# A new written order for a single-core kernel: DMA queue, PSUM banks and copy engines of a gated recurrence and its gated convolution layer

## The chip, the cores and the metric

One core of one Trainium2 chip runs the kernel. The time is device microseconds of that core, here as the median of several executions. Beside it stands the span: from the first to the last instruction of one execution that the hardware profiler recorded.

The engines are named as in the profile: PE (TensorE, matrix multiplications; PEld its weight loads), DVE (VectorE), ACT (ScalarE), POOL (GpSimd) and SP (SyncE, which here only issues DMAs). Each engine runs its own instructions in the order in which they were written and waits at semaphores for the others. DMAs are issued by SP in one queue and are carried out by 16 DMA engines.

## The reference

Two stages over x of shape (4, 6336, 256), 25,344 rows of 256 values. The first is a gated linear recurrence over the sequence, the second a layer that gates a projection by a causal convolution of width 5:

```python
sig_r = 1.0 / (1.0 + np.exp(-r_gate)); sig_i = 1.0 / (1.0 + np.exp(-i_gate))
a_t = np.exp(c * sig_r * np.log(a_base))
x_gated = np.sqrt(np.maximum(1.0 - a_t * a_t, 1e-06)) * sig_i * x
for t in range(S):
    h = a_t[:, t] * h + x_gated[:, t]
    y[:, t] = h
...
for k in range(K):
    gate_pre += conv_w[k][None, None, :] * yp[:, k:k + S, :]
out = (1.0 / (1.0 + np.exp(-gate_pre)) * (y @ w_val)) @ w_out
```

## The kernel before

The rows are cut into 51 windows (0 and 1 and 50 of 256 rows, the others of 512) and these into 28 chunks (CHUNKS: chunks 0 to 2, 26 and 27 hold one window, the others two). BATCHES joins chunks for the square root, GROUPS joins them for the transposes of the recurrence gate. All of this is the same before and after.

The schedule is a table of words, ORDER. A word such as `cv.12@6,7` calls the function `op_cv` for window 12 with the PSUM banks 6 and 7 (there are eight banks). The functions are called in the order of the table, so the table sets the order of each engine's instructions, of SP's queue, and which bank each product goes to; nothing else decides it. In the words, the first number is a window for lr, li, lx, pp, up, uv, xp, cv, tg, vl, gv, ou, cd, ca, st; a chunk for ta, tb, tr, ex, sq, sa, nt, xg, xt, sc; a batch for rt. They are:

- SP: `lr`, `li`, `lx` load 512 KB (256 KB for a small window) of r_gate, i_gate and x (L289); `st` stores a window of the output (L513); `s_wl` loads weights. The loads go into rings of four windows each (`place`, and `w % NX` for x), so a load of window w waits until window w-4 has been used: `lr` for `ta`, `li` for `tb`, `lx` for `up`. The output ring has four windows too.
- ACT: `ta` and `tb` the hyperbolic tangents of r and i (L307, L310), `ex` the exponential that gives a (L370), `rt` the square root of one batch (L397), `tg` the tangent of the convolution (L469), `ca` a copy of a finished window out of PSUM (L502), `sa` a square. `rt` needs another function table than the rest; the loop over ORDER puts a table load (L529) at each change.
- POOL: `pp` adds one to tb (L317), `up` multiplies by x (L329), `sq` squares a (L378).
- DVE: `xg` multiplies by the square root (L419), `sc` the scan (L450), `gv` gate times value (L482), `cd` the same copy as `ca` (L500), `uv` for a few windows the work of `up`.
- PE: `tr`, `nt`, `xt`, `xp` transposes (L354, L412, L428, L334), `cv` convolution (L462), `vl` value projection (L477), `ou` output projection (L492).

For one chunk the chain is lr, ta, tr, ex, sq, rt, nt, xg, xt, sc, then for each window cv, tg, gv, ou, a copy, st; and beside it li, tb, pp, up (with lx) into xg, and sc into vl and gv.

Which engine copies a finished window is a word of the table as well: `cd` or `ca`.

```python
            if eng == "D":
                nc.vector.tensor_copy(out=dst, in_=src)
            else:
                nc.scalar.copy(out=dst, in_=src)
...
        for word in ORDER.split():
            word, _, at = word.partition("@")
            name, *idx = word.split(".")
            if table.get(name, have) != have:
                have = table[name]
                nc.scalar.preload_act_table_set(have)
            emit[name](*[int(k) for k in idx], *[int(k) for k in at.split(",") if k])
```

Of the kernel before, what the change touches and what calls it, by code (L numbers as in the profile page):

```python
# [33 lines left out]
GROUPS = [[0], [1], [2], [3, 4], [5, 6], [7, 8], [9, 10], [11], [12], [13, 14], [15, 16], [17, 18], [19, 20], [21], [22],  # L34
    [23, 24], [25], [26], [27]]

ORDER = """
s_ident s_small s_kt s_diag lr.0 ta.0 lr.1 ta.1 li.0 tr.0.1@0 tb.0 pp.0 tr.0.0@1 ex.0.1 tr.1.0@2 tr.1.1@3 lr.2 ta.2
ex.1.0 tr.2.1@0 ex.1.1 ex.2.1 tr.2.0@2 lr.3 lr.4 lr.5 ex.0.0 ta.3 lr.6 ta.4 li.1 tr.3.1@0,1 lx.1 tb.1 sq.2.1 sq.1.1
sq.0.1 ex.2.0 li.2 tr.3.0@2,3 li.4 lx.0 li.3 tb.2 xp.1@4 sq.0.0 sq.1.0 sq.2.0 up.0 uv.1 lr.7 lr.8 ex.3.1 sq.4.1 ex.3.0  # L40
sq.3.0 lr.9 lr.10 lx.2 lx.4 s_wl.2 lx.3 li.5 li.6 s_wl.1 tb.3 s_wl.3 s_wl.0 ta.5 lx.5 ta.6 lr.14 rt.0 xp.2@2,3 nt.0@4
xg.0 xt.0@0,1 li.8 li.7 uv.2 rt.1 rt.2 nt.1@4 nt.2@5 xg.2 xg.1 pp.4 sq.3.1 sq.4.0 lx.6 rt.3 lr.11 tb.4 lr.12
tr.5.0@6,7 ex.5.0 xt.1@5,4 li.9 lr.13 sc.0.0 sc.0.1 pp.3 up.4 lx.8 nt.3@2,3 xt.2@0,1 sc.1.0 li.10 up.3 sc.1.1 xg.3
xt.3@2,3 tb.5 cv.1@4,5 sc.2.1 lx.7 sc.2.0 tg.1 cv.0@6,7 tg.0 tr.5.1@0,1 ex.5.1 s_wcast vl.1@4,5 sc.3.1 sc.3.0 xp.6@6,7
vl.0@0,1 nt.4@2,3 li.12 pp.5 ta.7 lr.16 sq.5.0 sq.6.0 up.5 li.11 ta.8 pp.8 uv.6 tb.6 gv.0 ou.0.0@0 lr.15 cv.2@6,7 tg.2
xg.4 tr.7.1@2,3 ex.7.1 cd.0.0 xt.4@1,0 st.0 gv.1 ou.1.0@4 cd.1.0 pp.7 tr.7.0@6,7 vl.2@4,5 ex.7.0 lx.10 sc.4.1 gv.2
cv.3@2,3 ou.2.0@4,5 vl.4@6,7 st.1 up.8 li.14 lr.18 up.7 sq.6.1 tb.7 lx.9 cd.2.0 tg.3 cv.4@2,3 ta.9 vl.3@4,5 lr.17
sc.4.0 cv.6@0,1 tg.4 gv.4 gv.3 ou.3.0@4,5 sq.7.1 st.2 sq.7.0 lr.20 sq.5.1 pp.12 ou.4.0@6,7 cd.4.0 rt.4 lx.11 li.13
lx.12 lr.19 pp.10 cd.3.0 up.10 st.3 st.4 cv.5@2,3 nt.5@4,5 tg.5 tg.6 xg.5 nt.6@6,7 pp.9 up.9 xg.6 lx.14 li.16 li.15
ta.10 lr.21 lr.22 xt.5@4,5 tb.8 lx.13 sq.8.1 pp.11 ta.11 lr.24 lr.23 vl.5@0,1 tr.9.1@6,7 sc.5.1 ex.9.1 sc.5.0 gv.5  # L50
xt.6@2,3 sc.6.0 tr.9.0@4,5 ex.9.0 vl.6@0,1 li.18 cv.7@6,7 li.17 gv.6 nt.7@4,5 up.11 up.12 tb.9 cv.8@0,1 tg.7 sc.6.1
ta.12 xg.7 ou.5.0@6,7 cd.5.0 tg.8 ou.6.0@2,3 li.20 lx.16 cv.9@4,5 cd.6.0 xt.7@0,1 pp.14 up.14 sq.9.1 pp.13 st.5
vl.7@2,3 sq.9.0 up.13 sc.7.0 ta.13 lx.15 tg.9 tb.10 st.6 li.19 lx.17 tr.12.1@6 vl.9@4,5 gv.7 gv.9 ou.7.0@2,3 cd.7.0
sq.10.1 ou.9.0@4,5 sc.7.1 cd.9.0 cv.10@2,3 lr.25 sq.10.0 sq.8.0 rt.5 pp.17 lr.26 st.7 vl.8@0,1 tr.12.0@7 gv.8 pp.16
nt.8@4,5 xg.8 pp.15 ex.12.1 nt.9@0,1 xt.8@4,5 up.15 up.16 tb.11 xg.9 tg.10 ou.8.0@0,1 ca.8.0 ex.12.0 st.9 lr.27 lx.18
sc.8.1 sc.8.0 tr.11.0@6 ex.11.0 cv.11@2,3 vl.11@0,1 tr.11.1@5 tg.11 gv.11 lx.20 lr.28 st.8 ex.11.1 lx.19 vl.10@6,7
li.21 li.22 xt.9@2,3 up.17 pp.18 pp.20 ta.14 li.24 li.23 cv.12@4,5 tg.12 sq.12.0 pp.19 lx.21 gv.10 sc.9.0 ou.11.0@0,1
# [12 lines left out]
ou.23.0@2,3 ca.23.0 cv.22@0,1 tg.22 pp.27 pp.28 up.27 up.28 st.23 li.33 lx.32 xg.15 sc.14.1 sc.14.0 sq.17.0  # L70
ou.21.0@6,7 ca.21.0 vl.22@2,3 lx.31 xt.15@0,1 gv.22 st.20 tb.17 li.36 li.35 cv.24@6,7 st.21 pp.30 sq.18.0 ta.20
sc.15.0 sc.15.1 sq.18.1 pp.29 cv.26@4,5 tg.24 tg.26 up.30 lr.44 up.29 lx.33 pp.31 sq.17.1 tr.19.0@2,3 ex.19.0
nt.16@6,7 vl.24@4,5 tb.18 xg.16 pp.32 up.32 lx.36 lx.34 tr.19.1@0,1 ou.22.0@2,3 ex.19.1 up.31 xt.16@6,7 gv.24 cd.22.0
cv.25@4,5 tg.25 st.22 sc.16.1 sc.16.0 ou.24.0@2,3 cd.24.0 tb.19 cv.27@0,1 lr.41 vl.26@4,5 gv.26 lr.43 vl.25@6,7
vl.27@2,3 gv.25 sq.19.1 sq.19.0 tg.27 gv.27 st.24 cv.28@0,1 ou.25.0@6,7 cd.25.0 lr.42 ou.26.0@4,5 pp.34 st.25 cd.26.0
ou.27.0@2,3 cd.27.0 rt.8 nt.17@6,7 xg.17 tr.21.1@4 vl.28@2,3 pp.36 tg.28 gv.28 ta.23 ex.21.1 ta.22 xt.17@6,7 sc.17.0
cv.30@0,1 tg.30 pp.33 up.34 sq.20.0 li.37 up.36 pp.35 up.33 lx.35 li.38 nt.18@2,3 sc.17.1 sq.21.1 sq.20.1 vl.30@4,5
tr.21.0@6 ex.21.0 tr.22.0@0 ex.22.0 xg.18 up.35 st.26 li.40 li.39 gv.30 tr.22.1@1 ex.22.1 tb.20 ou.28.0@6,7 xt.18@2,3
sq.22.1 sq.21.0 sq.22.0 cv.29@4,5 tg.29 cv.31@0,1 vl.29@4,5 tg.31 cd.28.0 vl.31@6,7 sc.18.1 sc.18.0 st.27 lx.37 st.28
lr.45 tb.21 lx.38 li.41 pp.40 pp.38 gv.29 lx.39 gv.31 nt.19@0,1 xg.19 lx.40 lr.46 pp.37 pp.39 up.37 up.38 up.39  # L80
ou.29.0@4,5 ou.30.0@2,3 rt.9 cd.30.0 ou.31.0@6,7 cd.31.0 st.30 li.42 cd.29.0 st.29 cv.33@0,1 xt.19@2,3 sc.19.0 sc.19.1
# [22 lines left out]
def kernel(  # L104
# [456 lines left out]
```

## Time and profile before

| | |
|---|---|
| median of 3 runs | 296.16 us (295.24 to 296.34) |
| the profiled execution: its own time | 295.84 us |
| its span | 293.7 us |
| mean granted TensorE clock | 0.988 |
| copies of a window from PSUM, 128x1024 | DVE x31, 1212 ns each; ACT x17, 1021 ns each |
| copies in all (with the small windows) | DVE 33, ACT 18 |
| HBM read, written | 78.39 MB, 25.95 MB |
| a 512 KB load, issue to landing, median | r 7.8, i 7.2, x 7.7 us |

The profile page gives, for the span, how long each engine was busy, then the same in 40 equal slices, the DMA queues, the chain of waits that ended last, and groups of instructions by source line with the idle time before them. A window view gives the same busy times for a stretch that one chooses; a timeline lists instructions with start and length. An engine that is busy for nearly all of a stretch bounds that stretch; where it is idle, what ended its wait is written behind it.

### The profile page before, as it was taken

The page shows a single profiled execution, that of the slowest core. Times are in us where ns is not written, and L with a number is a line of the kernel's source. Part 1 is how long each engine was busy: PE and PEld are TensorE (multiplying, and loading weights), DVE is VectorE, ACT ScalarE, POOL GpSimd, SP SyncE. Part 2 cuts the span into 40 slices and gives each one's busy share as a digit, 9 for nine tenths or more (in the row PEclk, how much of TensorE's full clock was granted, in tenths as well). Part 3 has the DMA queues.
Part 4 walks back from the last instruction along what each step waited for, and adds up shares of the span by engine and source line. Part 5 has one row for each costly group of instructions (what it writes and reads, how often), then busy time and mean ns, then how long its engine had stood idle before and what let it go on. Part 6 is the DMA issues. An engine that isn't in the chain of part 4 may idle for free.

```text
span 293.7 us, 6223 instructions
## 1 busy us (share of the span) xinstructions
PE 237.7 (81%) x2470; PEld 163.7 (56%) x2497; DVE 243.4 (83%) x211; ACT 276.1 (94%) x200; POOL 241.8 (82%) x161
## 2 busy tenths in 40 slices
PE   2263778777697899997969889888889998999993
PEld 1241555445364758566636657556648664767652
DVE  5000797857999899998999998999999999999981
ACT  4899999999999999999999999999999999999754
POOL 1559979999899979999998899999998999565300
PEclk9996899999999999999999999999999999999999
DMA  7899999999999999999998999999999999965336
GB/s 240 310 405 389 382 407 408 413 407 383 402 405 389 394 367 407 394 379 396 413 330 286 370 415 413 421 363 408 378 374 387 381 345 374 352 224 214 148 144 250
DMA packets 29995, 104.75 MB, mean 357 GB/s; under 512 B 3335, under 2 KB 3854, under 8 KB 29966
## 3 DMA queue, kind: packets, MB, share of 16 engines
q1 hardware_dynamic: 29952, 104.35, 92.6%
q8 instruction: 19, 0.31, 0.4%
q14 instruction: 10, 0.08, 0.1%
q10 hardware_dynamic: 14, 0.01, 0.0%
HBM read 78.39 MB, written 25.95 MB: 355 GB/s over the span
## 4 chain that ended last, share of the span: by engine, by line
ACT 33%; PE 20%; DMA 19%; issue 11%; DVE 9%; POOL 3%; SPq 2%; ACTq 0%; DVEq 0%; POOLq 0%
DMA xring<-in_x_dram 10%; ACT ering L397 7%; ACT aring L370 6%; ACT tgring L469 6%; ACT tbring L310 6%; PE banks L477 5%; DMA rring<-in_r_gate_dram 5%; PE banks L492 5%; PE banks L462 4%; ACT taring L307 3%; ACT L529 3%; DVE tgring L482 3%; PE banks L412 3%; DMA out_dram<-oring 3%; DVE oring L500 2%
## 5 line engine op out<-in xcount | busy, mean ns | idle before, releaser
L329 POOL TENSOR_TENSOR uring<-tbring,xring 128x1024 bf16<-128x1024 bf16 (+1 forms) x48 | 100.8, 2114 | 9.2 <-DMA xring<-in_x_dram 8.3
L450 DVE TENSOR_TENSOR_SCAN yring<-aring,yring,banks 128x1024 bf16<-128x1024 f32 (+5 forms) x54 | 106.1, 1988 | 2.1 <-PE banks L428 1.9
L378 POOL TENSOR_TENSOR ering<-aring 128x1024 f32<-128x1024 f32 (+2 forms) x54 | 91.4, 1712 | 10.5 <-ACT aring L370 10.5
L462 PE MATMUL banks<-yring,diag 64*64 64x512 bf16 (+7 forms) x1080 | 62.0, 361 | 4.0 <-ACT tgring L469 1.4
L482 DVE SCALAR_TENSOR_TENSOR tgring<-tgring,banks 128x1024 bf16<-128x1024 bf16 (+1 forms) x51 | 58.9, 1177 | 6.1 <-ACT tgring L469 4.5
L317 POOL TENSOR_SCALAR tbring<-tbring 128x1024 bf16<-128x1024 bf16 (+1 forms) x48 | 48.8, 1028 | 12.2 <-ACT tbring L310 11.9
L492 PE MATMUL banks<-wo,tgring 128*128 128x256 bf16 x396 | 51.1, 274 | 7.3 <-DVE tgring L482 6.3
L370 ACT ACTIVATE aring<-banks,khf 128x2048 f32<-128x2048 bf16 (+3 forms) x38 | 54.4, 1469 | 0.6 <-PE banks L354 0.6
L477 PE MATMUL banks<-yring,wv 128*128 128x512 bf16 (+7 forms) x189 | 47.9, 358 | 6.2 <-ACT tgring L469 2.2
L469 ACT ACTIVATE tgring<-banks 128x1024 bf16<-128x1024 f32 (+1 forms) x51 | 49.6, 1004 | 3.2 <-PE banks L462 3.0
L492 PEld LDWEIGHTS <-tgring 128*128 128x128 bf16 x396 | 41.5, 114 | 17.7 <-DVE tgring L482 12.5
L310 ACT ACTIVATE tbring<-iring 128x2048 bf16<-128x2048 f32 (+2 forms) x28 | 48.1, 1718 | 3.2 <-DMA iring<-in_i_gate_dram 3.2
L307 ACT ACTIVATE taring<-rring 128x2048 bf16<-128x2048 f32 (+2 forms) x28 | 48.0, 1721 | 1.8 <-DMA rring<-in_r_gate_dram 1.7
L397 ACT ACTIVATE ering<-ering 128x4096 bf16<-128x4096 f32 (+5 forms) x15 | 44.7, 3017 | 0.1
L462 PEld LDWEIGHTS <-diag 64*64 64x64 bf16 x1080 | 28.8, 106 | 27.8 <-issue 11.6
L354 PE MATMUL banks<-ident_b,taring 128*128 128x128 bf16 x396 | 30.1, 230 | 16.4 <-ACT taring L307 8.7
L419 DVE TENSOR_TENSOR uring<-banks,uring 128x2048 bf16<-128x2048 bf16 (+2 forms) x28 | 30.3, 1093 | 15.3 <-PE banks L412 14.0
L500 DVE COPY oring<-banks 128x1024 f32<-128x1024 f32 (+1 forms) x33 | 38.2, 1180 | 5.2 <-PE banks L492 5.1
L354 PEld LDWEIGHTS <-taring 128*128 128x128 bf16 x396 | 26.1, 103 | 22.1 <-issue 10.2
L477 PEld LDWEIGHTS <-wv 128*128 128x128 bf16 x216 | 19.5, 97 | 25.9 <-issue 12.6
L412 PE MATMUL banks<-ident,ering 128*128 128x128 f32 x198 | 29.1, 290 | 5.7 <-ACT ering L397 3.2
L412 PEld LDWEIGHTS banks<-ident,ering 128*128 128x128 f32 x198 | 26.0, 207 | 11.2 <-ACT ering L397 6.0
(43 smaller groups left out, 126.3 us busy)
## 6 DMA issues: line engine op xcount, KB each, us to landing
rring<-in_r_gate_dram SPq DMA_DIRECT2D x48, 512.0 KB, 7.8
iring<-in_i_gate_dram SPq DMA_DIRECT2D x48, 512.0 KB, 7.2
xring<-in_x_dram SPq DMA_DIRECT2D x48, 512.0 KB, 7.7
out_dram<-oring SPq DMA_DIRECT2D x48, 512.0 KB, 5.1
rring<-in_r_gate_dram SPq DMA_DIRECT2D x3, 256.0 KB, 3.0
iring<-in_i_gate_dram SPq DMA_DIRECT2D x3, 256.0 KB, 5.4
xring<-in_x_dram SPq DMA_DIRECT2D x3, 256.0 KB, 5.1
out_dram<-oring SPq DMA_DIRECT2D x3, 256.0 KB, 6.4
```

The costliest lines, as they stand in the source:

```text
L310: nc.scalar.activation(**tangent(c, tbring, NTI, iring, NII))
L329: nc.gpsimd.tensor_tensor(out=u, in0=t1, in1=xt, op=ALU.mult)
L370: nc.scalar.activation(out=dst, in_=src, func=ACT.Exp, scale=khf[:, h:h + 1], bias=khf[:, h:h + 1])
L378: nc.gpsimd.tensor_tensor(out=e, in0=a, in1=a, op=ALU.mult)
L397: nc.scalar.activation(out=ering[:].bitcast(BF16)[:, 4 * o:4 * o + 2 * n], in_=ering[:, 2 * o:2 * o + 2 * n], func=ACT.Sqrt, scale=-0.25, ...
L412: nc.tensor.transpose(out=bank[:, k:k + P], in_=ering[:, e + q:e + wins[w] // 2:nq], identity=ident[:])
L450: nc.vector.tensor_tensor_scan(out=yring[:, h, col:col + o1 - o0], data0=aring[:, h, a_at[c] + o0:a_at[c] + o1], data1=xT[:, o0:o1], initi ...
L462: nc.tensor.matmul(out=gp[oh * 64:oh * 64 + 64, h, a:b], lhsT=diag[half * 64:half * 64 + 64, h, k, :], rhs=yring[half * 64:half * 64 + 64, ...
L469: nc.scalar.activation(out=tgring[:, w % NTG, :, 0:wins[w]], in_=live.pop(("gp", w))[:, :, 0:wins[w]], func=ACT.Tanh, scale=0.5)
L477: nc.tensor.matmul(out=val[:, m, a:b], lhsT=wv[:, hk, m * P:(m + 1) * P], rhs=yring[:, hk, col:col + b - a], start=(hk == 0), stop=(hk == ...
L482: nc.vector.scalar_tensor_tensor(out=tgring[:, w % NTG, :, 0:wins[w]], in0=tgring[:, w % NTG, :, 0:wins[w]], scalar=1.0, in1=live.pop(("va ...
L492: nc.tensor.matmul(out=ops[:, j * D:(j + 1) * D], lhsT=gv[:, hk, j:wins[w]:J], rhs=wo[:, hk, :], start=(hk == 0), stop=(hk == H - 1))
```

## The change

ORDER is replaced. It has 961 words before and after, and the same operations on the same windows, with two kinds of difference: the order of the words and the bank numbers behind the @, and the copying engine of five windows. Windows 8, 21, 33 and 35 were copied by ACT (`ca`) and are now copied by DVE (`cd`); window 5 was copied by DVE and is now copied by ACT. So DVE has 36 copies for 33, and ACT 15 for 18. The number of table loads stays 18. CHUNKS, BATCHES and GROUPS are only wrapped differently, so line numbers after them are higher by one. The table, cut to its beginning, its end and the words that the prediction names:

```diff
@@ -31,72 +31,73 @@
 ORDER = """
-s_ident s_small s_kt s_diag lr.0 ta.0 lr.1 ta.1 li.0 tr.0.1@0 tb.0 pp.0 tr.0.0@1 ex.0.1 tr.1.0@2 tr.1.1@3 lr.2 ta.2
-ex.1.0 tr.2.1@0 ex.1.1 ex.2.1 tr.2.0@2 lr.3 lr.4 lr.5 ex.0.0 ta.3 lr.6 ta.4 li.1 tr.3.1@0,1 lx.1 tb.1 sq.2.1 sq.1.1
-sq.0.1 ex.2.0 li.2 tr.3.0@2,3 li.4 lx.0 li.3 tb.2 xp.1@4 sq.0.0 sq.1.0 sq.2.0 up.0 uv.1 lr.7 lr.8 ex.3.1 sq.4.1 ex.3.0
-sq.3.0 lr.9 lr.10 lx.2 lx.4 s_wl.2 lx.3 li.5 li.6 s_wl.1 tb.3 s_wl.3 s_wl.0 ta.5 lx.5 ta.6 lr.14 rt.0 xp.2@2,3 nt.0@4
-xg.0 xt.0@0,1 li.8 li.7 uv.2 rt.1 rt.2 nt.1@4 nt.2@5 xg.2 xg.1 pp.4 sq.3.1 sq.4.0 lx.6 rt.3 lr.11 tb.4 lr.12
...
-cv.3@2,3 ou.2.0@4,5 vl.4@6,7 st.1 up.8 li.14 lr.18 up.7 sq.6.1 tb.7 lx.9 cd.2.0 tg.3 cv.4@2,3 ta.9 vl.3@4,5 lr.17
-sc.4.0 cv.6@0,1 tg.4 gv.4 gv.3 ou.3.0@4,5 sq.7.1 st.2 sq.7.0 lr.20 sq.5.1 pp.12 ou.4.0@6,7 cd.4.0 rt.4 lx.11 li.13
...
-ta.12 xg.7 ou.5.0@6,7 cd.5.0 tg.8 ou.6.0@2,3 li.20 lx.16 cv.9@4,5 cd.6.0 xt.7@0,1 pp.14 up.14 sq.9.1 pp.13 st.5
...
-nt.8@4,5 xg.8 pp.15 ex.12.1 nt.9@0,1 xt.8@4,5 up.15 up.16 tb.11 xg.9 tg.10 ou.8.0@0,1 ca.8.0 ex.12.0 st.9 lr.27 lx.18
...
-ou.21.0@6,7 ca.21.0 vl.22@2,3 lx.31 xt.15@0,1 gv.22 st.20 tb.17 li.36 li.35 cv.24@6,7 st.21 pp.30 sq.18.0 ta.20
...
-tr.23.0@0,1 gv.34 xt.20@4,5 lx.42 tb.23 pp.43 up.41 ex.23.0 ou.33.0@6,7 ca.33.0 sc.20.1 sc.20.0 cv.35@2,3 tg.35
...
-li.45 ta.27 sq.23.0 tr.25.1@0 tr.25.0@1 nt.22@2,3 ca.35.0 up.42 ex.25.0 sq.23.1 lx.44 pp.44 up.44 sq.25.0 sq.24.0
...
-sc.21.0 cv.39@4,5 lx.43 tg.39 up.43 cd.36.0 vl.37@0,1 lx.46 sc.22.0 lx.45 gv.37 rt.10 vl.38@6,7 gv.38 ou.37.0@0,1
-ou.38.0@6,7 sc.22.1 cd.38.0 cv.40@4,5 cd.37.0 tg.40 li.48 vl.39@2,3 gv.39 st.36 nt.23@6,7 pp.46 up.45 up.46 li.47
-tb.25 pp.48 pp.47 lr.49 ta.26 lx.47 st.37 st.38 li.49 li.50 xg.23 vl.40@0,1 gv.40 nt.24@2,3 xg.24 xt.23@6,7 sc.23.1
-ou.39.0@4,5 ca.39.0 tr.27.0@0 tr.27.1@1 ex.27.1 ex.27.0 lx.50 lx.48 cv.42@2,3 up.47 tg.42 st.39 cv.41@4,5 tg.41
-sc.23.0 up.48 ou.40.0@0,1 ca.40.0 st.40 sa.27.1 vl.41@2,3 gv.41 vl.42@4,5 gv.42 tr.26.1@6 sq.27.0 tr.26.0@7 ex.26.0
-xt.24@0,1 sc.24.0 ex.26.1 sq.26.1 sc.24.1 tb.26 pp.49 sq.26.0 ou.41.0@2,3 ca.41.0 cv.43@4,5 cv.44@6,7 vl.43@2,3 tg.43
-ou.42.0@4,5 tg.44 rt.11 st.41 lx.49 nt.25@6,7 ca.42.0 gv.43 vl.44@0,1 xg.25 ou.43.0@2,3 xt.25@6,7 ca.43.0 gv.44
-cv.46@4,5 tb.27 tg.46 cv.45@2,3 tg.45 sc.25.1 sc.25.0 st.42 ou.44.0@0,1 ca.44.0 nt.26@7 st.43 st.44 up.49 xg.26
-vl.46@4,5 gv.46 vl.45@2,3 gv.45 cv.47@0,1 tg.47 ou.46.0@4,5 ca.46.0 xt.26@6,7 sc.26.0 ou.45.0@0,1 vl.47@2,3 ca.45.0
-st.45 nt.27@4 cv.48@5,6 tg.48 sc.26.1 cv.49@0,1 tg.49 gv.47 pp.50 up.50 xg.27 xt.27@5,4 sc.27.1 vl.49@2,3 ou.47.0@6,7
-ca.47.0 st.46 vl.48@0,1 gv.49 ou.49.0@2,3 ca.49.0 sc.27.0 st.47 cv.50@6,7 tg.50 gv.48 st.49 ou.48.0@0,1 ca.48.0 st.48
-vl.50@2,3 gv.50 ou.50.0@2 ca.50.0 st.50
+s_ident s_small s_kt s_diag lr.2 lr.0 s_wl.3 lr.1 li.0 lr.3 s_wl.2 ta.2 ta.0 lr.4 tr.0.1@0 ta.1 lr.6 tr.2.0@1 tb.0
+lr.5 tr.1.0@2 tr.0.0@3 tr.2.1@4 ex.2.0 li.1 tr.1.1@5 li.2 ex.1.1 li.3 ex.0.1 sq.1.1 lx.0 ex.1.0 li.4 sq.2.0 ex.0.0
+ex.2.1 sq.1.0 ta.3 sq.2.1 pp.0 sq.0.0 ta.4 sq.0.1 tb.1 lr.10 tr.3.0@4,5 tb.2 lr.9 lr.8 tr.3.1@2,3 lr.7 ex.3.0 lx.2
+s_wl.1 up.0 lx.1 ex.3.1 sq.3.0 lx.4 lx.3 tb.3 sq.3.1 ta.6 pp.4 sq.4.1 lr.13 ta.5 li.5 li.6 sq.4.0 li.7 xp.2@2,3
+lr.14 pp.3 rt.0 tr.5.0@4,5 lx.6 uv.2 rt.2 up.4 nt.0@0 rt.1 xg.0 rt.3 xt.0@0,1 xp.1@2 sc.0.0 up.3 nt.1@3 lx.5 nt.2@0
...
+pp.8 xt.4@2,3 gv.4 st.3 sq.7.1 li.11 lr.18 sc.4.1 ou.4.0@0,1 li.13 lx.9 up.8 rt.4 sc.4.0 pp.9 up.7 cd.4.0 cv.6@2,3
+st.4 vl.6@0,1 lx.12 pp.10 li.14 nt.5@4,5 lx.11 sq.8.0 cv.5@6,7 tg.6 xg.5 tb.7 up.10 gv.6 xt.5@4,5 ou.6.0@0,1 sc.5.0
+ta.9 li.16 up.9 vl.5@2,3 tg.5 lr.19 cd.6.0 ta.10 pp.11 nt.6@6,7 gv.5 st.6 pp.12 li.15 xg.6 tb.8 ou.5.0@2,3 lr.22
+up.11 tr.9.0@0,1 sc.5.1 ca.5.0 xt.6@6,7 ex.9.0 st.5 tr.9.1@2,3 lr.20 sc.6.0 lr.21 cv.7@4,5 ex.9.1 sq.8.1 up.12
...
+tr.11.1@4 sc.7.1 st.9 up.16 lr.25 cd.10.0 cv.11@2,3 up.13 cd.8.0 st.10 nt.8@0,1 lr.23 tr.11.0@5 st.8 pp.15 xg.8
+tg.11 vl.11@6,7 lr.24 lx.18 ex.11.1 up.15 xt.8@0,1 gv.11 lx.17 ex.11.0 nt.9@2,3 sc.8.0 sq.11.1 tb.10 cv.12@6,7
...
+nt.14@2,3 up.27 lx.29 li.31 ta.18 lr.36 lx.30 cd.21.0 vl.22@0,1 lr.35 xg.14 pp.28 tg.22 tr.17.1@6,7 up.28 lr.38
...
+up.39 ta.23 gv.34 ou.33.0@6,7 pp.41 ta.24 xg.21 lr.48 xt.20@0,1 lr.47 pp.42 st.31 cd.33.0 cv.35@4,5 lx.42 tg.36
...
+st.34 sq.23.1 cv.38@4,5 lx.44 sc.21.1 tg.37 tr.25.1@6 up.42 ex.25.1 nt.22@2,3 cd.35.0 tg.38 ou.36.0@6,7 sq.24.0
+xg.22 sa.25.1 st.35 tr.25.0@0 lr.50 vl.38@4,5 lx.46 ex.25.0 cd.36.0 pp.43 xt.22@2,3 tb.24 gv.38 st.36 sq.25.0
+cv.39@6,7 lx.45 sc.22.0 vl.39@4,5 tg.39 li.47 pp.46 vl.37@0,1 lr.49 up.43 ou.38.0@6,7 gv.37 rt.10 li.48 cd.38.0
+ou.37.0@0,1 pp.45 sc.22.1 vl.40@6,7 up.44 gv.39 cv.40@2,3 up.46 cd.37.0 nt.23@4,5 st.37 cv.41@0,1 xg.23 tg.40 up.45
+lx.48 st.38 lx.47 ta.27 tg.41 nt.24@2,3 gv.40 vl.41@4,5 xg.24 ta.26 tr.27.0@0 xt.23@6,7 gv.41 ex.27.0 ou.39.0@2,3
+tb.25 sc.23.0 cv.42@4,5 ca.39.0 ou.41.0@0,1 pp.48 tg.42 sc.23.1 st.39 xt.24@2,3 pp.47 li.49 ca.41.0 li.50 tr.26.0@6
+ou.40.0@4,5 up.48 ex.26.0 st.41 tr.26.1@0 sc.24.0 tr.27.1@1 ca.40.0 cv.44@6,7 ex.27.1 up.47 st.40 cv.43@4,5 ex.26.1
+lx.49 sc.24.1 tg.44 sa.27.1 nt.25@0,1 sq.26.1 tg.43 vl.42@6,7 sq.27.0 tb.26 xg.25 vl.44@4,5 sq.26.0 tb.27 vl.43@2,3
+gv.42 pp.50 xt.25@0,1 pp.49 gv.44 ou.42.0@6,7 rt.11 gv.43 ou.44.0@4,5 up.49 ca.42.0 sc.25.1 ou.43.0@2,3 ca.44.0
+st.42 cv.45@6,7 ca.43.0 st.44 cv.46@4,5 sc.25.0 st.43 lx.50 nt.26@1 tg.46 vl.46@2,3 xg.26 tg.45 cv.47@4,5 gv.46
+vl.47@6,7 tg.47 ou.46.0@2,3 gv.47 up.50 vl.45@4,5 ca.46.0 nt.27@6 ou.47.0@0,1 gv.45 st.46 xt.26@2,3 ca.47.0 xg.27
+ou.45.0@4,5 sc.26.0 st.47 cv.48@0,1 ca.45.0 sc.26.1 xt.27@6,7 st.45 tg.48 vl.48@4,5 sc.27.1 cv.49@2,3 gv.48
+vl.49@0,1 tg.49 sc.27.0 ou.48.0@4,5 gv.49 cv.50@2,3 ca.48.0 ou.49.0@0,1 tg.50 st.48 vl.50@4,5 ca.49.0 gv.50 st.49
+ou.50.0@4 ca.50.0 st.50
 """
```

## The prediction

> **What bounds the kernel now.** First the page: busy times of the whole span, then its 40 slices.
>
> ```profile
> span 293.7 us, 6223 instructions
> PE 237.7 (81%) x2470; PEld 163.7 (56%) x2497; DVE 243.4 (83%) x211; ACT 276.1 (94%) x200; POOL 241.8 (82%) x161
> ...
> DVE  5000797857999899998999998999999999999981
> ACT  4899999999999999999999999999999999999754
> ...
> DMA  7899999999999999999998999999999999965336
> ```
>
> ACT is idle for 293.7 - 276.1 = 17.6 us only. The window view tells where (columns: stretch, its length, busy us and instructions of each engine, granted clock, DMA share, GB/s):
>
> ```profile
> 0.00:27.64 27.64, 9.32 (x54) 6.24 (x55) 4.54 (x21) 22.05 (x21) 14.31 (x20) 0.94 0.90 334
> ...
> 69.20:251.60 182.40, 159.01 (x1706) 111.04 (x1725) 175.13 (x132) 181.14 (x119) 174.87 (x105) 1.00 1.00 382
> ...
> 250.20:293.70 43.50, 38.64 (x403) 26.86 (x408) 35.42 (x30) 33.48 (x37) 15.28 (x12) 1.00 0.58 220
> ```
>
> So there are three stages. A head of 27.64 us, up to the first square root, in which ACT is idle for 5.6 us and waits for loads (below). A body, to the end of rt.10 at 250.2, in which ACT has no gaps to speak of (1.3 us idle of 182.4) and sets the pace; the DMA engines are full and DVE has 7.3 us left, 4%. A tail of 43.5 us in which PE, 38.64 us busy, is the bound, and ACT follows it.
>
> ACT's timeline gives the marks (start, length; last bracket: idle time before, and what ended it):
>
> ```profile
> 7.06 0.63 ACT L310 ACTIVATE tbring<-iring 128x512 bf16<-128x512 f32 x1 [2.28 <-DMA iring<-in_i_gate_dram]
> ...
> 14.30 1.91 ACT L307 ACTIVATE taring<-rring 128x2048 bf16<-128x2048 f32 x1 [0.95 <-DMA rring<-in_r_gate_dram]
> ...
> 27.64 1.28 ACT L529 ACT_TABLE_LOAD   x1
> ```
> ```profile
> 234.29 0.69 ACT L307 ACTIVATE taring<-rring 128x512 bf16<-128x512 f32 x1
> ...
> 244.88 5.33 ACT L397 ACTIVATE ering<-ering 128x6144 bf16<-128x6144 f32 x1
> ...
> 268.61 1.90 ACT L502 COPY oring<-banks 128x1024 f32<-128x1024 f32 x2
> ```
>
> The wait views, DVE's in the body and SP's own (waiter <- releaser: us, times, longest), show what follows the busy engines about:
>
> ```profile
> DVE uring L419 <- PE banks L412: 4.6, 6, 1.5
> ```
> ```profile
> SPq L513 <- DVE oring L500: 60.3, 22, 5.3
> ```
>
> **The change part by part.**
>
> Copies off ACT. Four `ca` go, one comes, all between rt.4 and rt.10. Two in a row take 1.90 us, so one is worth 0.95 in a gapless queue: 3 x 0.95 = 2.85. Also ta.27 (0.69, less the overlap some 0.62) moves from before rt.10 to behind it. By both, rt.10 ends 3.5 us earlier, if ACT stays without gaps. Two more tangents, tb.7 and ta.9 (1.9 each, together 3.7), move from before rt.4 to behind it, so the gain is had early: rt.4 ends 3.7 earlier, and from there to rt.10 ACT has 182.6 us to do for 182.4.
>
> The head. Up to rt.0 ACT does the same twenty activations in another order, ta.2 first. Loads in SP's queue up to the last one that it needs: before, 15.0 units of 512 KB (to lr.10, for ta.6), after 14.75 (to lr.7, for ta.5). At 410 GB/s, which the full slices show, a unit takes 1.28 us; if the DMA engines stay the bound, the gain is 0.25 x 1.28 = 0.3. They lost about 1 us before, because lr.6 waited for ta.2 and held li.1 behind it; after, ta.2 runs first and nothing is held until lr.10, which waits for ta.4. With no such hole I place ta.4's end at 15.4: lr.10 cannot land before 15.4 + 2.7 (the shortest landing of an r load) = 18.1, and ACT reaches ta.6 at 22.8, so loads are early and the table load comes at 26.5, 1.1 us sooner. I take 0.5, between 0.3 and 1.1. Bounds: the 5.6 us of idle time are all that could be had, less the 2.7 that the first load takes and the extra 0.64 of a first load of double size, so 2.3 at most; at worst -1, a wait like the 0.95 above.
>
> Copies onto DVE. Three more at 1.21 us (31 of them took 36.8 us in union, 1.19 each): 3 x 1.19 = 3.6. In the body DVE then has 175.1 + 3.6 = 178.7 to do in ACT's 182.6, and 3.9 us of room for 7.3. What can't shrink are the waits of L419 for the transposes that follow each square root, 4.6 us in six; with the 0.3 of the scans' waits for banks 4.9, 1.0 more than the room. So 1.0 is charged. Bounds: 0 (all absorbed) and 7.3 - 3.9 = 3.4 (none).
>
> The other engines' orders, and banks. POOL keeps its 241.8 us, PE its work; a bank comes back into use after three or more PE operations in 235 of 260 cases, before in 230 of 260: as tight, no price, from -1 to +1. For the loads I compared ACT's work ahead of each `ta` and `tb` with the units ahead of its loads: in the body most loads stand earlier against their use than before (tb.6 by 7 us, ta.9 by 8; only ta.19 by 7 later, which had 12 in hand). No price.
>
> The tail, walked by the rows from the end of rt.10 as 0. Before, the last copy ends at 290.7 - 250.2 = 40.5. After: transposes nt.23 to 1.2, xg.23 2.5, gv.40, xg.24 4.9, gv.41 6.1, then four scans of 2.3 in a row to 15.3; PE waits for the second of them (10.7) with cv.44, and has done ou.43 at 21.2, where before the same set of work was done at 20.9. sc.25 ends at 24.7, cv.47 26.2, gv.47 28.5, xg.27 30.5, three scans to 33.8, gv.48 35.0, sc.27.0 35.8, cv.50 37.2, tg.50 38.1, gv.50 39.4, ou.50 40.1, last copy 40.7. The small last load of x (lx.50) stands behind st.43 and so behind a copy that ends at 23.0; up.50 then ends at 27.7, 2.3 before xg.27 needs it: hidden, and if it landed 2.3 later, not. Price 0.2; from -1.5 to +2.
>
> Sum, against the profiled execution: 293.7 - 3.5 - 0.5 + 1.0 + 0.2 = 290.9 us span. Its time was 295.84, so 2.1 lie around the span: 293.0. The median of the runs is 0.3 above that execution: 293.3 us, 1.0% less.
>
> **The rivals.**
>
> DVE becomes the bound. For it: DVE is 96% busy in the body, and 178.7 of 182.6 would be 98%. Against it: much of its idle time is order, not need. If it keeps all 7.3 us of idle time, the body takes 178.7 + 7.3 = 186.0, 3.6 more than the 182.4 before; the head and the early rt.4 still give 0.5 + 3.7: 293.7 - 4.2 + 3.6 + 0.2 = 293.3, or 295.7 us: no change. The Trainium skill's page Perfetto Trace Analysis, section Optimizing Scalar/DVE Operations, says that work which either engine can do may be moved to Scalar when DVE is saturated; the change does the reverse. Its rule points to this rival, while the row has ACT fuller still, at 99%.
>
> Slower: stores hold the loads. SP issues in order, and stores wait at its head for DVE's copies, 60.3 us in 22 waits, 2.7 each, the longest 5.3. After, st.8, st.21, st.33 and st.35 wait for a DVE with less room; lr.24, li.34 or lr.50 stand behind them. If each held SP for 5.3, 2.6 more, and the loads behind had 1.0 in hand (lr.20, behind ca.5, is let go 8.8 us of ACT work before its use, and an r load lands in 7.8), ACT would lose 4 x 1.6 = 6.4: 290.9 + 6.4 = 297.3, or 299.7 us. It decides the sign from a hold of 4.8 us: 4 x (4.8 - 3.7) = 4.4, which brings 293.3 to 297.7. For it: before, POOL waits 8.3 us for x loads and ACT 4.9 for r and i, so margins are thin. Against it: the loads stand earlier.
>
> **How the numbers follow.** Forecast 0.56 (291 to 294.6), DVE the bound 0.20, held loads 0.24. Runs of this kernel tell 0.5% from no change, that is 294.7 to 297.6. So faster 0.56, same 0.20, slower 0.24. The range, 290.0 to 298.8, has at its low end the tail and the head at their good bounds without DVE's charge (span 290.9 - 1.0 - 1.7 - 0.6 = 287.6, or 290.0 us), and takes in most of the held loads.
>
> **What would show it.** Right: ACT busy 273.2, with x15 copies, and DVE 247.0; the first table load near 27.1; ACT idle in the body by no more than 2.5 us; rt.10 ending at 247.2, and the last copy 40.7 later. Wrong: ACT's `tg` or `ex` waiting for PE in the body (DVE late), `ta` and `tb` waiting for loads with SP held at L514 (stores), or a tail above 42.

## The result, and the profile after

| | before | after |
|---|---|---|
| median, 15 runs each | 295.98 us (293.97 to 297.99) | 294.42 us (292.83 to 295.48) |
| ratio to before | | 0.9951, interval 0.993 to 0.9972 |
| the profiled execution: its own time | 295.84 us | 294.79 us |
| its span | 293.7 us | 292.8 us |

The new order is faster by 0.5%, where 1.0% was forecast: 294.4 us for 293.3, inside the range. First the page of the changed kernel (line numbers are higher by one than before):

```profile
span 292.8 us, 6228 instructions
PE 241.5 (83%) x2473; PEld 166.1 (57%) x2497; DVE 246.9 (84%) x214; ACT 274.1 (94%) x197; POOL 241.8 (83%) x161
...
DVE  5001799766999999999999999979999999999891
ACT  5999979999799999999999999999999999999754
...
PEclk9999999968999999999997999999999999999999
```

ACT's work fell from 276.1 to 274.1 (273.2 was forecast) and DVE's rose from 243.4 to 246.9 (247.0). But the span fell by 0.9 only, so ACT is idle a microsecond longer than before: its row has a 7 in the sixth slice (36.6 to 43.9 us) and one in the eleventh (73.2 to 80.5). In the granted clock there is a 6 in the ninth slice, from 58.6 us on.

The windows, to be read against the three of before (length, busy us and instructions of PE, PEld, DVE, ACT, POOL, granted clock, DMA share, GB/s):

```profile
0.00:26.52 26.52, 7.04 (x52) 5.75 (x53) 3.80 (x20) 22.18 (x21) 14.83 (x20) 1.00 0.95 353
...
64.10:249.20 185.10, 164.90 (x1739) 113.57 (x1748) 177.10 (x135) 182.03 (x117) 179.12 (x109) 0.98 1.00 388
...
249.20:292.80 43.60, 38.82 (x401) 26.11 (x404) 35.22 (x29) 34.18 (x37) 17.14 (x13) 1.00 0.62 226
```

The first table load comes at 26.52 for 27.64. Between the ends of rt.4 and rt.10 ACT has 182.03 us to do, and the stretch takes 185.1: 3.1 us idle. Before, the same stretch took 182.5 with 181.24 busy and 1.3 idle:

```profile
67.70:250.20 182.50, 158.98 (x1704) 111.17 (x1724) 173.84 (x132) 181.24 (x119) 175.01 (x106) 1.00 1.00 383
```

The forecast's 182.6 us to do was worked out from the length of a stretch, 182.4, and so had its idle 1.3 us in it; counted from the 181.24 of work, the same moves give 181.4, and ACT had 0.6 more. By stretches, with the ends of the square roots as marks (us; "again" is a second profile of the same order, "repaired" the version y_tb4_warm below):

| stretch | before | forecast | after | again | repaired |
|---|---|---|---|---|---|
| start to rt.0 | 29.6 | 29.1 | 28.4 | 28.1 | 27.7 |
| rt.0 to rt.4 | 38.1 | 34.4 | 35.7 | 35.0 | 35.4 |
| rt.4 to rt.10 | 182.5 | 183.7 | 185.1 | 184.9 | 183.0 |
| rt.10 to the last copy | 40.5 | 40.7 | 40.6 | 40.7 | 40.6 |

(Forecast: 250.2 - 3.5 - 0.5 + 1.0 = 247.2 for rt.10, less 67.7 - 3.7 - 0.5 = 63.5 for rt.4, is 183.7.)

Where ACT waits shows in its own timeline (last bracket: idle time before, and what ended it):

```profile
37.85 2.06 ACT L371 ACTIVATE aring<-banks,khf 128x2048 f32<-128x2048 bf16 x1 [1.06 <-PE banks L355]
...
41.12 0.60 ACT L470 ACTIVATE tgring<-banks 128x512 bf16<-128x512 f32 x1 [0.71 <-PE banks L463]
...
76.32 1.01 ACT L503 COPY oring<-banks 128x1024 f32<-128x1024 f32 x1 [1.78 <-PE banks L493]
```

These are ex.5.1, tg.1 and ca.5, the one copy that the change moved to ACT. What made the last of them late stands in the timelines of PE and DVE:

```profile
62.43 2.35 PE L463 MATMUL banks<-yring,diag 64*64 64x512 bf16 x20 [3.43 <-DVE yring L451]
64.71 1.89 PE L478 MATMUL banks<-yring,wv 128*128 128x512 bf16 x4
66.39 1.74 PE L413 MATMUL banks<-ident,ering 128*128 128x128 f32 x8
```
```profile
68.24 1.23 DVE L420 TENSOR_TENSOR uring<-banks,uring 128x2048 bf16<-128x2048 bf16 x1 [4.75 <-PE banks L413]
```

PE waits 3.43 us for a scan. Behind the wait the granted clock is 0.50 (the window from 63 to 66 us), and the convolution cv.6, the value product vl.6 and the transposes nt.5 take 2.35, 1.89 and 1.74 us, where the same three take 1.28, 1.04 and 1.11 at a clock of 1.00 (x_warm, below). DVE, which needs nt.5 for xg.5, stands 4.75 us; ou.5 starts at 75.2, and ACT waits for it with ca.5 at the head of its queue and everything else behind.

### The profile page after: what moved, and what is told of

Same layout as the page of the kernel before. It is cut to its first block, busy times and chain, and to the rows that moved or that the text cites. A ratio compares the mean times of both kernels' runs of the same rounds, so it can differ in the third digit from the quotient of the medians.

```text
span 292.8 us, 6228 instructions
## 1 busy us (share of the span) xinstructions
PE 241.5 (83%) x2473; PEld 166.1 (57%) x2497; DVE 246.9 (84%) x214; ACT 274.1 (94%) x197; POOL 241.8 (83%) x161
## 4 chain that ended last, share of the span: by engine, by line
POOL 33%; PE 30%; DVE 16%; issue 10%; DMA 7%; ACT 3%; SPq 1%; DVEq 0%; POOLq 0%; ACTq 0%
POOL uring L330 14%; POOL ering L379 12%; PE banks L463 9%; DVE yring L451 7%; POOL tbring L318 7%; PE banks L493 5%; PE banks L478 5%; PE banks L413 4%; DVE tgring L483 4%; DMA rring<-in_r_gate_dram 4%; DMA xring<-in_x_dram 3%; DVE oring L501 2%; PE banks L355 2%; PE banks L335 2%; PE banks L429 2%
## 5 line engine op out<-in xcount | busy, mean ns | idle before, releaser
L463 PE MATMUL banks<-yring,diag 64*64 64x512 bf16 (+7 forms) x1080 | 63.9, 366 | 7.0 <-DVE yring L451 6.4
L470 ACT ACTIVATE tgring<-banks 128x1024 bf16<-128x1024 f32 (+1 forms) x51 | 50.6, 1007 | 3.7 <-PE banks L463 3.6
L478 PE MATMUL banks<-yring,wv 128*128 128x512 bf16 (+4 forms) x192 | 49.6, 368 | 2.4 <-ACT tgring L470 0.3
L501 DVE COPY oring<-banks 128x1024 f32<-128x1024 f32 (+1 forms) x36 | 42.1, 1186 | 1.6 <-PE banks L493 1.1
L355 PE MATMUL banks<-ident_b,taring 128*128 128x128 bf16 x396 | 31.2, 234 | 9.3 <-ACT taring L308 7.5
L420 DVE TENSOR_TENSOR uring<-banks,uring 128x2048 bf16<-128x2048 bf16 (+2 forms) x28 | 30.5, 1094 | 9.3 <-PE banks L413 8.5
L355 PEld LDWEIGHTS <-taring 128*128 128x128 bf16 x396 | 27.1, 106 | 15.9 <-ACT taring L308 9.5
L413 PE MATMUL banks<-ident,ering 128*128 128x128 f32 x198 | 30.5, 298 | 2.7 <-ACT ering L398 2.2
L478 PEld LDWEIGHTS <-wv 128*128 128x128 bf16 x216 | 20.2, 99 | 21.5 <-issue 7.5
L413 PEld LDWEIGHTS banks<-ident,ering 128*128 128x128 f32 x198 | 26.6, 208 | 9.7 <-ACT ering L398 3.9
```

The source lines that it names most:

```text
L355: nc.tensor.transpose(out=bank[:, o:o + P], in_=taring[:, place(w, NTR), j, h * P:(h + 1) * P], identity=ident_b[:])
L413: nc.tensor.transpose(out=bank[:, k:k + P], in_=ering[:, e + q:e + wins[w] // 2:nq], identity=ident[:])
L463: nc.tensor.matmul(out=gp[oh * 64:oh * 64 + 64, h, a:b], lhsT=diag[half * 64:half * 64 + 64, h, k, :], rhs=yring[half * 64:half * 64 + 64, ...
L470: nc.scalar.activation(out=tgring[:, w % NTG, :, 0:wins[w]], in_=live.pop(("gp", w))[:, :, 0:wins[w]], func=ACT.Tanh, scale=0.5)
L478: nc.tensor.matmul(out=val[:, m, a:b], lhsT=wv[:, hk, m * P:(m + 1) * P], rhs=yring[:, hk, col:col + b - a], start=(hk == 0), stop=(hk == ...
```

## The experiments

All ratios are to the kernel before, run beside it on the same chip. T1 and T2 are the theories that each expectation names; all runs but the last four were meant to tell where the gain of the copies had gone.

### The copy of window 5 back on DVE (x_cd5)

```diff
-ca.5.0
+cd.5.0
```

> The new order with one word changed: window 5 is copied by DVE again (cd.5.0 for ca.5.0). Theory 1 (ACT sets the pace; its copy of window 5 waits 1.78 us for PE in the new profile, and takes 0.95): rt.5 ends 2.0 to 2.7 us earlier than in the new order (at 94.4 to 95.1 for 97.1), and the time is 0.986 to 0.990 of the kernel before, where the new order had 0.995. Theory 2 (DVE, now with a 37th copy, or POOL sets the pace): 0.995 or more.

Measured: 297.06 us, 1.0043 (1.0014 to 1.0073). Not faster but 0.9% slower than the new order: taking the waiting instruction off ACT is no repair. Its one profile has a span of 482.9 us and doesn't stand for these times, so the reason is read from x_oldcopies, which has the same copy on DVE.

### The old copy engines in the new order (x_oldcopies), and the new ones in the old order (b_newcopies)

```diff
 x_oldcopies, in the new order
-ca.5.0 ... cd.8.0 ... cd.21.0 ... cd.33.0 ... cd.35.0
+cd.5.0 ... ca.8.0 ... ca.21.0 ... ca.33.0 ... ca.35.0
 b_newcopies, in the old order
-cd.5.0 ... ca.8.0 ... ca.21.0 ... ca.33.0 ... ca.35.0
+ca.5.0 ... cd.8.0 ... cd.21.0 ... cd.33.0 ... cd.35.0
```

> The new order with all five copies on the engine of the kernel before (5 on DVE; 8, 21, 33, 35 on ACT). Theory 1 (ACT sets the pace): ca.5 with its wait goes (-2.0 to -2.7 us), four copies of 0.95 come (+3.8): 1.1 to 1.8 us longer than the new order, 0.999 to 1.001 of before. Theory 2 (DVE sets the pace, three copies less there): 2 to 3.6 us shorter than the new order, 0.983 to 0.988.

> The order before with the copying engines of the new one, each at its old place in the table (8, 21, 33, 35 on DVE; 5 on ACT). Theory 1 (ACT sets the pace and the copies are the larger part of the gain): 0.990 to 0.995 of before. Theory 2 (DVE has no room for them in an order not made for them; its scans come late behind the copies): 1.000 to 1.010.

Measured: x_oldcopies 299.33 us, 1.0127 (1.008 to 1.0175); b_newcopies 300.23 us, 1.0146 (1.0097 to 1.0194). Both halves alone are slower than before, more than either theory allowed; only together they are faster. The windows of the two from rt.4 to rt.10:

```profile
63.10:252.80 189.70, 164.06 (x1739) 113.11 (x1748) 174.58 (x132) 184.51 (x119) 179.34 (x109) 0.99 0.99 379
```
```profile
68.10:255.10 187.00, 159.65 (x1704) 111.71 (x1724) 177.35 (x136) 179.36 (x115) 176.75 (x106) 1.00 0.98 375
```

ACT's busy time moves as counted, somewhat less: three copies more cost it 184.51 - 182.03 = 2.5 us, three less spare 181.24 (the kernel before, between the same marks) - 179.36 = 1.9, so 0.6 to 0.8 a copy for the 0.95 assumed. But its idle time is 5.2 and 7.6 us, for 3.1 and 1.3 with the engines that belong to the order. x_oldcopies shows how, in the timelines of ACT and PE:

```profile
76.22 2.06 ACT L371 ACTIVATE aring<-banks,khf 128x2048 f32<-128x2048 bf16 x1 [2.69 <-PE banks L355]
79.81 2.06 ACT L371 ACTIVATE aring<-banks,khf 128x2048 f32<-128x2048 bf16 x1 [1.54 <-PE banks L355]
```
```profile
74.22 1.07 PE L493 MATMUL banks<-wo,tgring 128*128 128x256 bf16 x8 [1.69 <-DVE tgring L483]
75.12 1.06 PE L355 MATMUL banks<-ident_b,taring 128*128 128x128 bf16 x16
76.02 1.04 PE L429 MATMUL banks<-ident,uring 128*128 128x128 f32 x8
78.72 1.05 PE L355 MATMUL banks<-ident_b,taring 128*128 128x128 bf16 x16 [1.66 <-DVE oring L501]
```

These are two different waits. The exponential ex.9.0 (76.22) waits for the first transposes, tr.9.0 (75.12), which need no bank of that copy: they follow ou.5 (74.22) without a gap, and ou.5 is late. That is the wait that ca.5 met in the new order; with ca.5 gone from ACT, ex.9.0 meets it, and in both runs it starts 13.1 us behind the end of rt.4. So nothing is won there. The second transposes, tr.9.1 (78.72), write into ou.5's banks 2 and 3. The copy on DVE (L501) empties them only behind a scan, at 78.67, where ca.5 had done so at 77.33, and ex.9.1 waits another 1.54 us. In b_newcopies there are two waits as well: ex.25.0, ahead of which the copy of window 35 had stood, waits 2.14 us at 239.25 for transposes that follow ou.35, and cv.38 waits 1.30 at 241.54 for the banks of that copy (L500), so that its `tg` waits 1.32 at 242.88. The engine of a copy decides when two of the eight banks come free, and taking a copy from ACT wins nothing where the next instruction waits as long. These are the longest of ACT's waits between rt.4 and rt.10 in the two runs; what the others cost was not taken apart.

### The head alone (b_head)

```diff
 in the old order
-s_diag lr.0 ta.0 lr.1 ta.1 li.0 ... lr.2 ta.2
+s_diag lr.2 ta.2 lr.0 ta.0 lr.1 ta.1 li.0 ...
```

> The order before with one part of the new head: lr.2 and ta.2 first, so that lr.6, which waits for ta.2, no longer holds li.1 and the loads behind it. Theory 1 (the head's gain of the new order, 1.1 us at rt.0, comes from this and is kept to the end): the first table load 0.5 to 1.1 us earlier than before (26.5 to 27.1), the time 0.996 to 0.998 of before. Theory 2 (the body's DMA and POOL set their own pace and eat it): the table load is earlier, the end is not, 0.999 to 1.001.

Measured: 294.74 us, 0.9965 (0.9931 to 0.9999). The profiled span is 293.0; rt.0 ends at 28.5 for 29.6 before, rt.10 at 249.6 for 250.2, the last copy at 290.0 for 290.7. So this part of the change alone, one load and one tangent moved to the front, measures 0.35% for the whole change's 0.49%. Eight profiles with the new head as it is end rt.0 at 27.5 to 28.4, the two with the old one at 29.0 and 29.6: the means differ by 1.4 us, for the 0.5 forecast.

### Keeping the clock up (x_warm)

```diff
 in the new order
-cv.6@2,3
+wm.40@6 cv.6@2,3
+        def op_wm(n, *at):
+            bank = banks[:, at[0]].bitcast(BF16)
+            for k in range(n):
+                nc.tensor.transpose(out=bank[:, k % 8 * P:(k % 8 + 1) * P], in_=ident_b[:], identity=ident_b[:])
```

> The new order with 40 extra transposes of the identity on PE, into bank 6, which is free there, ahead of cv.6, in the 3.4 us in which PE waits for a scan; nothing else is changed. Theory 1 (PE's clock falls to 0.5 after that wait, so that cv.6, vl.6 and nt.5 take 2.35, 1.89 and 1.74 us, and the copy ca.5 comes late): the granted clock stays 1.0 at 62 to 66 us, cv.6 takes 1.3, xg.5 starts 1.5 to 2.0 earlier, ACT's wait before ca.5 falls from 1.78 to under 0.4, and the time is 0.989 to 0.991 of before. Theory 2 (another engine sets the pace, ACT's wait is slack): the clock stays up, the time remains at 0.995. Theory 3 (cv.6 is slow for another reason): cv.6 still takes over 2 us.

Measured: 293.4 us, 0.9922 (0.9891 to 0.9953). Forty transposes whose results nobody reads fill 2.4 us of PE's wait, in PE's timeline:

```profile
57.73 2.40 PE L520 MATMUL banks<-ident_b 128*128 128x128 bf16 x40
61.32 1.28 PE L463 MATMUL banks<-yring,diag 64*64 64x512 bf16 x20 [1.19 <-DVE yring L451]
```

PE still waits for the same scan, and cv.6 starts 1.7 us ahead of the end of rt.4, as in the new order. But the clock stays at 1.00, cv.6 takes 1.28, ACT's wait before ca.5 is gone, and rt.4 to rt.5 takes 31.0 us for 33.0. So the loss at ca.5 came from the clock, not from the late scan. The intervals of the two times overlap; the marks do not. With these fillers rt.4 to rt.5 takes 31.0 us in three profiles of three, and without them, ca.5 being on ACT, 31.9 to 33.0 in six. The two shortest of the six, 31.9 (x_skipca) and 32.1 (y_headwarm), are those in which the slow products came back to full speed soonest (vl.6 in 1.34 us, nt.5 in 1.27), and ca.5 waited 0.65 and 0.92. Part of the gain went again later: the clock fell in this profile to 0.62 between 211 and 214 us, and two `tg` waited 0.57 and 1.07 us.

### A tangent moved to where ACT waits (x_tb4)

```diff
-ex.5.1 ... tg.1 tb.4
+tb.4 ex.5.1 ... tg.1
```

> The new order with tb.4 moved ahead of ex.5.1 on ACT, where ACT waits 1.06 us for tr.5.1 and then 0.71 for the convolution. Theory 1 (each gap of ACT before rt.10 is lost for good): both gaps filled, li.9 and li.10, which wait for tb.4, issued 4 to 5 us earlier, rt.4 1.2 to 1.8 us earlier, the time 0.989 to 0.991 of before for the new order's 0.995. Theory 2 (the gain is eaten at ca.5.0, which waits for PE after its slow stretch at 62 to 68 us): rt.4 earlier, rt.5 not, ACT's wait before ca.5.0 longer than 1.78, the time 0.994 to 0.996.

Measured: 293.61 us, 0.992 (0.9889 to 0.9951). The wait of ex.5.1 is gone, but tg.2 then waits 0.89 for PE, and rt.0 to rt.4 takes 35.1 us, as in the second profile of the unaltered order (35.0). ca.5 still waits 1.62. The time points to a gain; its place in the profile does not.

### Copies left out (x_skipca, x_skipcd)

```diff
 x_skipca
-ca.23.0 ... ca.34.0
 x_skipcd
-cd.8.0 ... cd.21.0 ... cd.33.0 ... cd.35.0
```

> The new order without ca.23 and ca.34: windows 23 and 34 of the output are not copied (their stores write what the ring held). ACT has 1.9 us less to do in the body. Theory 1 (ACT sets the body's pace): 1.5 to 1.9 us shorter than the new order, 0.988 to 0.990 of before. Theory 2 (POOL, through which the chain of waits runs from 109 to 223 us, or DVE stands right behind it): 0 to 0.6 us shorter, 0.993 to 0.995, and ACT idle 1.3 us or more longer.

> The new order without cd.8, cd.21, cd.33 and cd.35: these four windows are not copied (their stores write what the ring held). DVE has 4.8 us less to do, ACT the same. Theory 1 (ACT sets the pace; the copies fit into DVE's room): within 0.5 us of the new order, 0.994 to 0.997 of before. Theory 2 (the copies cost the body 1 us or more through DVE, as the prediction charged): 1.0 to 3.4 us shorter, 0.984 to 0.992.

Measured: x_skipca 293.32 us, 0.9911 (0.9881 to 0.9942); x_skipcd 294.0 us, 0.993 (0.9904 to 0.9957). Against the new order's 0.9951, two copies less on ACT give 0.4%, or 1.2 us of the 1.9 counted, between the theories; rt.7 to rt.8, with one copy less, takes 35.3 us for 35.8, so that copy was worth 0.5. But rt.9 to rt.10, with the other copy less, takes 34.9 us for 33.6: in this profile the clock fell at 211 us (shown in the last section) and two `tg` waited 0.59 and 1.07 us. (In x_warm, with the same fall and every copy, it takes 35.2.) Four less on DVE, 4.1 us of its work (242.8 busy for 246.9), bring the body nothing: rt.5 to rt.10 takes 152.5 us for 152.1. Here are the windows from rt.5 to rt.10, first of the new order, then of x_skipcd:

```profile
97.10:249.20 152.10, 135.74 (x1460) 94.23 (x1468) 148.69 (x116) 150.91 (x99) 147.91 (x91) 0.99 1.01 393
```
```profile
95.40:247.90 152.50, 136.83 (x1474) 94.47 (x1468) 144.58 (x112) 151.01 (x97) 147.85 (x91) 0.99 1.01 392
```

DVE went from 148.69 to 144.58 us and ACT stayed at 151, all but 1.5 us of the stretch. DVE at 98% was not the bound: that an engine is busy for nearly all of a stretch does not by itself make it the bound there.

### Warming the head, both repairs, and the order again (y_headwarm, y_tb4_warm, y_all, y_again)

```diff
 y_headwarm
-xp.2@2,3
+wm.80@6 xp.2@2,3
 y_tb4_warm: x_tb4 and x_warm together
 y_all: y_tb4_warm, and
-xp.2@2,3 ... ou.31.0@0,1
+wm.80@6 xp.2@2,3 ... wm.25@4 ou.31.0@0,1
```

> The new order with 80 filler transposes into PSUM bank 6 (free then, overwritten later) ahead of xp.2, in TensorE's 7.9 us wait for the x of the sample group. T1 (a half clock right behind that wait makes the first products late, and the activations ex.5.1 and tg.1 wait 1.06 + 0.71 us for them before rt.4): xp.2's four passes take about 2.0 us for 3.75, rt.4 ends 1.0 to 1.7 us earlier than 64.1, and it is kept to the end: ratio to before 0.989 to 0.992, where the new order alone had 0.995. T2 (what is won there is taken back in ScalarE's wait at ca.5): 0.994 to 0.996.

> Both single repairs of the new order together: tb.4 ahead of ex.5.1 (0.992 alone) and 40 filler transposes ahead of cv.6 (0.992 alone). T1 (the two losses are separate waits of ScalarE, so the repairs add): rt.5 ends at 92.5 to 93.5 and the ratio to before is 0.987 to 0.989. T2 (the next low clock or GpSimd's own work takes the second gain): 0.991 to 0.993.

> The two repairs, the 80 fillers ahead of xp.2, and 25 fillers into bank 4 ahead of ou.31.0 (the wait of 2.37 us at 210 us behind which the clock dropped in two of the runs). T1 (each loss is a wait of ScalarE for a TensorE that is late by its clock or its place): 0.985 to 0.988. T2 (only one of them can be won, then GpSimd's work or the loads decide): 0.991 to 0.993.

> The new order unchanged, on the same chip as the three variants of it. Both theories: ratio to before 0.993 to 0.997; its marks (rt.4 near 64, rt.5 near 97, rt.10 near 249) say which of the waits come in every execution: T1 expects the waits of ex.5.1 and of ca.5 for TensorE (1.06 and 1.78 us) again, T2 (a chance dip of the clock in one profiled execution) expects the wait at ca.5 to be under 0.5 us.

Measured:

| | median us | ratio, interval | span | rt.4 to rt.5 | wait at ca.5 |
|---|---|---|---|---|---|
| y_again | 294.16 | 0.9951 (0.992 to 0.9983) | 291.7 | 32.9 | 1.67 |
| y_headwarm | 294.82 | 0.9964 (0.9934 to 0.9994) | 291.3 | 32.1 | 0.92 |
| y_tb4_warm | 293.07 | 0.9908 (0.9873 to 0.9943) | 289.6 | 31.0 | none |
| y_all | 291.86 | 0.9873 (0.9835 to 0.9911) | 290.9 | 31.0 | none |

(The last three columns are of one profiled execution each. Its own time was 293.62, 293.31, 291.67 and 292.98 us; in y_tb4_warm it was the shortest of eight, 1.4 below the median.)

The order again gives the same ratio and the same wait at ca.5, so that is no chance of one execution. In y_tb4_warm the clock is 1.00 from rt.4 to rt.10, and ACT does rt.4 to rt.10 almost without gaps:

```profile
63.00:246.00 183.00, 162.71 (x1747) 112.07 (x1745) 177.11 (x135) 181.73 (x117) 178.38 (x108) 1.00 1.01 392
```

183.0 us for 185.1, 1.3 idle for 3.1: as little idle time as before the change, and 0.7 better than the forecast with its charge for DVE. The loads are the same, and the DMA engines, whose share was 1.00 in the slower stretch too, bring them at 392 GB/s for 388; so it was not they that held the new order back here. Whether the two repairs add is not settled by the times: 0.9908 lies between the theories and its interval covers both. The profile gives what was won to the fillers: rt.0 to rt.4, where the moved tangent stands, takes 35.4 us, no less than in y_again (35.0), and rt.5 ends at 94.0, for T1's 92.5 to 93.5.

y_headwarm does what T1 says at its place: xp.2 takes 1.96 us for 3.75, the waits of ex.5.1 and tg.1 are gone, and rt.3 to rt.4 takes 28.8 us for 30.0 in y_again. But in that profile the head had ended 1.6 us later than in y_again, behind a wait of 2.98 us for a load of r, and the time shows no gain. Since the fillers touch no load I take this for scatter of the first loads, without a run that shows it.

y_all has the best time measured, 1.3% less than before. Its interval overlaps that of y_tb4_warm, and its profile, whose own time was above its median (292.98), shows no gain over it: there the 80 fillers didn't hold the clock, and xp.2 took 3.31 us after a wait of 2.69. That y_all beats both given kernels is shown; that it beats y_tb4_warm is not.

## Why the prediction was right, and where not

Copies off ACT. Right in kind: ACT is busy for 150.91 of 152.10 us from rt.5 to rt.10, and with two copies less on it the time is shorter (x_skipca), by 1.2 of the 1.9 us, though the intervals overlap. The size was over: 0.6 to 0.8 us of work a copy for 0.95, which had been read from two copies in a row; so ACT had 182.03 us to do from rt.4 to rt.10 for the 181.4 counted. And the condition "if ACT stays without gaps" is the step that failed: ACT was idle there for 3.1 us, more than the 2.5 named as the limit, and rt.10 came 1.0 us earlier, not 3.0 (3.5 and 0.5, less 1.0).

The tangents behind rt.4. rt.4 came 3.6 us earlier for the 3.7 and 0.5 forecast, but only with the head's larger gain. From rt.0 to rt.4 the step had 3.7 and got 2.4, and 3.1 in the second profile; ACT's work there fell by 3.5 (37.39 to 33.86), and its idle time rose by 1.1, and by 0.4 in the second profile. That idle time is its waits for PE at ex.5.1 and tg.1 (1.06 + 0.71, then 0.36 + 0.72). With the tangents gone from there, ACT reached these two before PE did. I had checked the loads against the earlier use, not PE's products.

The head. Mis-sized: 0.5 taken, some 1.4 measured (1.1 in b_head alone). The walk over the ring had given 1.1 as the upper value, and I went below it for the DMA engines' sake; their share in the head rose from 0.90 to 0.95 and did not hold it.

DVE. The charge of 1.0 and the rival "DVE becomes the bound" fell with x_skipcd: 4.1 us of DVE work less did not shorten the body. The added work found room in gaps: between 97.1 and 249.2 us DVE is busy for 148.69 us, and was for 145.32 before, at the same ACT work (150.91 and 150.92). This is the stretch before the change:

```profile
97.10:249.20 152.10, 135.90 (x1479) 95.19 (x1495) 145.32 (x112) 150.92 (x101) 145.56 (x88) 1.00 0.99 381
```

So the waits of L419 (L420 after), which I had kept as a floor under DVE's idle time, were no floor: in this stretch they fell from 3.1 us in five waits to 1.8 in two. By the Trainium skill's page Perfetto Trace Analysis, section Optimizing Scalar/DVE Operations, work may go from a saturated DVE to ScalarE; here ScalarE was the fuller one. In b_newcopies and x_oldcopies neither direction paid without the order and banks made for it.

Banks and other orders, "no price, from -1 to +1". This is the other side of the failed condition, and where the 2 us went that rt.4 to rt.5 lost: PE's own order gave it a wait of 3.43 us, the clock fell behind it, and through nt.5, xg.5 and ou.5 it reached ACT at ca.5. That x_warm takes the loss away and leaves the scan where it is shows the clock as the cause. The sign I had named for being wrong, `tg` or `ex` waiting for PE in the body, is the form that it took, but not by DVE's extra copies, the nearest of which, cd.8, comes later. I had no rival with the clock in it, though PE's waits in the trace of before (1.38 and 1.65 us between 58 and 64 us, at a clock of 1.00) were there to be compared with the new order's.

Stores holding loads did not come: the list of ACT's waits shows none for a load after rt.0. Of the signs named for it, SP stood behind st.6 until 74.06 us and behind st.5, with ca.5 late, until 77.36, and DMA moved 250 GB/s from 72 to 75 us, but no tangent waited for it.

The tail: 40.6 for the 40.7 walked.

So 292.8 for a span of 290.9 is: head 0.7 better, rt.0 to rt.4 1.3 worse, rt.4 to rt.10 1.4 worse, tail 0.1 better. The time came as near as it did by luck: errors of opposite sign met. The charge of 1.0 for DVE, which was not needed, also hid part of the miss in the body; without it the forecast from rt.4 to rt.10 would have been 182.7 for the 185.1 measured. And by its time b_head, two words moved, gets 0.35 of the 0.49%, though the intervals of the two overlap.

## What to carry to other kernels

Where one engine is full, a copy taken from it is worth at most its length, and less or nothing if the PSUM bank is freed later or the next instruction waits as long; look who writes into that bank next, and what follows in the queue, before moving the copy. When an order makes TensorE wait for about 3 us (here 3.4 us cost the clock in seven of seven profiles, 2.4 in two of nine), price the products behind the wait at half clock, and follow them to the first instruction of the full engine that needs one: filler transposes in that wait were the cheapest repair here. Predict by stretches between marks, so that a gain in one and a loss in another don't hide each other.

## What the hardware did that I had not expected

The clock behind PE's waits. Before cv.6 it waited 3.42 or 3.43 us in seven profiles without fillers, and in all seven cv.6 ran slowly (1.93 to 2.35 us for 1.28), the products behind it in most; with fillers it waited 1.19 us, and in three of three they did not. A wait of 2.37 us before ou.31 stands in nine profiles, and the clock fell in two of them (the next convolution took 2.03 and 2.35 us for 1.27). First y_again, then x_skipca, in PE's timeline:

```profile
211.20 1.06 PE L493 MATMUL banks<-wo,tgring 128*128 128x256 bf16 x8 [2.37 <-DVE tgring L483]
212.20 1.27 PE L463 MATMUL banks<-yring,diag 64*64 64x512 bf16 x20
```
```profile
210.29 1.06 PE L493 MATMUL banks<-wo,tgring 128*128 128x256 bf16 x8 [2.37 <-DVE tgring L483]
211.28 2.03 PE L463 MATMUL banks<-yring,diag 64*64 64x512 bf16 x20
```

The same wait, the same products, and 1.27 us in one execution for 2.03 in the other. The Trainium skill's page TensorE: Matmul & The Clock Gate, section Part 1: The HAM clock gate (the "warmup" mystery), has the clock fall to half after an idle window of about 3.4 us, and the window run free of the kernel. The 3.43 us are about as long as that window, but a window that runs free would seldom lie whole within a wait no longer than itself, and here the clock fell in seven of seven. A wait of 2.37 us is shorter than that window and yet cost the clock in two of nine. So the rule of the Trainium skill by itself gives neither count, and what sets them stays open.

The clock's record isn't always the clock. In the new order xp.2's four passes took 3.75 us with a recorded clock of 1.00 from 26 to 30 us, and in y_again the same 3.75 us with 0.50 recorded from 26 to 28; in y_headwarm they took 1.96. Durations of a known product tell more than the row.
